# Retention taken two chunks at a time, with four input tiles in place of three

## The chip, the cores and the metric

The kernel runs on one core of a Trainium2 chip. A core has a matrix engine (TensorE, PE in the profile; its weight loads are shown apart, as PEld), a vector engine (VectorE, DVE), a scalar engine (ScalarE, ACT), GpSimd (POOL) and a sync engine (SP) that issues most of the transfers. Each engine runs its own list of instructions in order and waits on semaphores for the others. The metric is the time of one execution on the device, in microseconds; the median of several runs is compared.

## The reference

Three stages follow one another. The first is a retention (a linear attention with decay) over q, k, v of shape 2 x 8 x 768 x 64, in float32; then a feed-forward layer on the 1536 tokens, then a mixture of 8 experts whose gate is normalised eight times over.

```python
for t in range(S):                       # S = 768
    state = gamma * state + einsum('bhd,bhe->bhde', k[:, :, t], v[:, :, t])
    y[:, :, t] = scale * einsum('bhd,bhde->bhe', q[:, :, t], state)
x = y as (1536, 512)
h = x @ w_in;  g = h * clip(h + 3, 0, 6) / 6;  x = g @ w_out
out = sum over experts e of  P[:, e] * (relu(x @ w1[e]) @ w2[e])   # P: gate, 8 rounds of normalisation
```

## The kernel before

The change touches the retention alone, which is the first 54 us of 1268. The two batches are cut into 6 chunks of 128 tokens each, 12 chunks in all, numbered 0 to 11; chunks 0 and 6 begin a batch. For each chunk there are two input tiles of 512 KB: qk (queries and keys with the head dimension on the rows, four pairs of heads) and kv (keys and values with the tokens on the rows). The work of one chunk n is:

- scores: 16 matmuls, keys against queries, on 64 rows of the array each, two side by side, into the PSUM banks s0 and s1; VectorE multiplies both by the decay mask into two tiles a (L391).
- within: 16 matmuls of a with the values, 64 columns of the array each, two side by side, into a bank y (L416).
- across: 8 matmuls of the full array, the scaled queries qs with the copied state rs of the chunks before, added into the same y (L422). A batch's first chunk has none.
- state: 8 matmuls of the full array, scaled keys ks with the values, added into one PSUM bank r for the whole batch (L401); ScalarE copies the diagonal blocks to rs, one of two tiles that take turns (L407). A batch's last chunk has none.
- GpSimd makes ks from kv (L375) and qs from qk (L368).
- keep empties y: ScalarE writes the rounded high part (L309), VectorE the difference as low part (L311), and from chunk 4 on ScalarE copies y a second time into tiles b11 to b22 (the list late, L429).

Each of the PSUM tags s0, s1, y and r has two banks that take turns. The instructions are given in a hand-written order, and each engine's list follows it. Beside the retention VectorE and ScalarE split the 64-bit weights of the feed-forward layer into two parts; pump(n) puts n such steps (one VectorE operation each: L243, L155, L248, L175 in turn) at that place of the order, and the step at L155 asks for the next raw tile on SP's queue. The list HP says how many steps go with each chunk, 18 in all.

Before, the loop goes chunk by chunk: scores of chunk n + 1, its qs, the loads of qk, then within, across, keep and state of chunk n, ks of chunk n + 1, the load of kv, and pump. The scores thus run one chunk ahead. qk and kv have three buffers each, so a load waits on SP until the tile three chunks earlier has been used. After the loop comes the dense stage, whose first matmuls are at L483: x0 with the split weights into banks s0, then x1 into banks y, and the second product into acc (L587).

Of the kernel before, what the change touches and what calls it, by code (L numbers as in the profile page):

```python
# [23 lines left out]
NPAIR = H // 2  # L24
NCB = S // P
NCH = B * NCB
# [20 lines left out]
TURN = (4, 9, 14)  # L47
GATE = lambda it, at: 16 * it + at > 7 and (16 * it + at) % 24 in (2, 8, 14, 19)
APART = 3
KVB = 3  # L50
QKB = 3
WARM = 12
HP = (1, 1, 1, 2, 2, 1, 1, 2, 2, 2, 2, 2)
AHEAD = 3
RAWS = (0, 2)
GF = 4
NGR = F1T // GF
PLAIN = 1
# [6 lines left out]
def kernel(  # L65
# [11 lines left out]
    nc = tc.nc  # L77
# [5 lines left out]
    def bank(tag, name=None):  # L83
        return ps_s.tile([P, BLK], F32, tag=tag, name=name or tag)

    by_pair = lambda t: t.rearrange("p (h i) -> p h i", h=NPAIR)
# [17 lines left out]
    wg_raw = const.tile([P, KT, E], F32, name="wg_raw")  # L104
# [28 lines left out]
    def load_w(tag=None):  # L133
        unit = next(raw_next, None)
        if unit is None:
            return
        i, part = unit
        tags[unit] = tag = tag or next(ring["raw"])
        t = sp.tile([P, 2 * BLK], U32, tag=tag, name="raw")
        nc.sync.dma_start(out=t, in_=wf_in[i, :, part * BLK:(part + 1) * BLK].bitcast(U32))  # L140
        raw_t[unit] = t
# [130 lines left out]
    def rounded():  # L272
        while later:
            later.pop(0)()
# [3 lines left out]
    def pump(n):  # L278

        for _ in range(n):  # L280
            rounded()
            if not next(split_next, False):
                break
            state_["pumped"] += 1
# [17 lines left out]
    def keep(n, y):  # L302

        b, at_ = divmod(n * P, BLK)
        cs = slice(at_, at_ + P)
        pieces = [(x0[0], x0[1], y)] if b == 0 else [(x1[0], x1[1], y)] if b == 1 else [
            (x3[0], x3[1], y[:, 0:2]), (x2[0], x2[1], y[:, 2:4])]
        for hi, lo, src in pieces:
            nc.scalar.activation(out=hi[:, :, cs], in_=src, func=AF.Copy)  # L309
        for hi, lo, src in pieces:  # L310
            nc.vector.tensor_tensor(out=lo[:, :, cs], in0=src, in1=f32(hi[:, :, cs]), op=ALU.subtract)  # L311
        if b:
            late.extend((t[:, :, cs], y[:, 2 * k:2 * k + 2]) for k, t in enumerate(((b11, b21), (b12, b22))[b - 1]))
# [4 lines left out]
    qk_t, kv_t, qs_t, ks_t, a_t, acc_r = {}, {}, {}, {}, {}, {}  # L318
# [5 lines left out]
    rs = [at1.tile([P, NPAIR, P], F32, name=f"rs{i}") for i in range(2)]  # L324

    def load_qk(n):
        if n < NCH:
            qk_t[n] = at2.tile([P, 2, NPAIR, P], F32, tag="qk", name="qk", bufs=QKB)
            nc.sync.dma_start(out=qk_t[n], in_=qk_in[n])

    def spread(tag, to, row):

        t = by_pair(bank(tag, "dm"))
        nc.tensor.matmul(
            t.rearrange("p h i -> p (h i)"), tab[:, to * P:(to + 1) * P], tab[:, TO + row * BLK:TO + (row + 1) * BLK],
            start=True, stop=True,
        )  # L340
        return t
# [13 lines left out]
    def query_table(c, tag):  # L355

        nc.scalar.activation(out=tq[:, c - 1], in_=spread(tag, 2, c), func=AF.Copy)

    def load_kv(n):
        if n < NCH:  # L360
            kv_t[n] = at2.tile([P, 2, DM], F32, tag="kv", name="kv", bufs=KVB)
            nc.sync.dma_start(out=kv_t[n], in_=kv_in[n])

    def scale_q(n):
        c = n % NCB
        if c and n < NCH:
            t = at2.tile([P, NPAIR, P], F32, tag="qs", name="qs")
            nc.gpsimd.tensor_tensor(out=t, in0=qk_t[n][:, 0], in1=tq[:, c - 1], op=ALU.mult)  # L368
            qs_t[n] = t

    def scale_k(n):
        c = n % NCB
        if c < NCB - 1:
            t = at2.tile([P, DM], F32, tag="ks", name="ks")
            nc.gpsimd.tensor_tensor(  # L375
                out=t.rearrange("p (h d) -> p h d", h=H), in0=kv_t[n][:, 0].rearrange("p (h d) -> p h d", h=H),
                in1=gk[:, c].rearrange("p (h o) -> p h o", o=1).to_broadcast([P, H, D]), op=ALU.mult,
            )
            ks_t[n] = t

    def scores(n):
        if n >= NCH:
            return
        t = [by_pair(bank(f"s{j}", "sc")) for j in range(2)]
        for p in range(NPAIR):
            for j in range(2):
                r = slice(j * D, (j + 1) * D)
                nc.tensor.matmul(t[j][:, p], qk_t[n][r, 1, p], qk_t[n][r, 0, p], start=True, stop=True)  # L388
        for j in range(2):
            a_t[n, j] = a = at2.tile([P, NPAIR, P], F32, tag="a", name="a", bufs=4)  # L390
            nc.vector.tensor_tensor(out=a, in0=t[j], in1=dmask[:, j], op=ALU.mult)  # L391

    def state(n):
        b, c = divmod(n, NCB)
        if c == NCB - 1:
            return
        if c == 0:
            acc_r[b] = by_pair(bank("r"))
        for p in range(NPAIR):
            cs = slice(p * P, (p + 1) * P)  # L400
            nc.tensor.matmul(  # L401
                acc_r[b][:, p], ks_t[n][:, cs], kv_t[n][:, 1, cs],
                start=(c == 0 and p == 0), stop=True, skip_group_check=True,
            )
        for j in range(2):
            r = slice(j * D, (j + 1) * D)
            nc.scalar.activation(out=rs[n % 2][r, :, r], in_=acc_r[b][r, :, r], func=AF.Copy)  # L407

    def attend(n):
        c = n % NCB  # L410

        y = by_pair(bank("y"))
        for p in range(NPAIR):
            for j in range(2):
                h = 2 * p + j
                nc.tensor.matmul(  # L416
                    y[j * D:(j + 1) * D, p], kv_t[n][:, 1, h * D:(h + 1) * D],
                    a_t[n, j][:, p], start=(p == 0), stop=(c == 0), skip_group_check=True,
                )
        if c:  # L420
            for p in range(NPAIR):
                nc.tensor.matmul(  # L422
                    y[:, p], rs[(n - 1) % 2][:, p], qs_t[n][:, p],
                    start=False, stop=True, skip_group_check=True,
                )
        keep(n, y)
        state(n)
        for t, src in late:
            nc.scalar.activation(out=t, in_=src, func=AF.Copy)  # L429
        late.clear()  # L430
# [776 lines left out]
    with tc.manual_schedule():  # L1207
# [4 lines left out]
        load_kv(0)  # L1212
        load_kv(1)
        load_qk(2)
        load_w()
        load_kv(2)
        nc.vector.memset(rs[0][:, 0], 0.0)
        nc.vector.memset(rs[0][:, 1:], 0.0)
        nc.vector.memset(rs[1], 0.0)
# [13 lines left out]
        scale_k(0)  # L1233
        for c in (2, 3):
            query_table(c, "y")
        for n in range(NCH):
            scores(n + 1)
            if n == 0:
                for c in range(4, NCB):
                    query_table(c, "r")  # L1240
            scale_q(n + 1)
            if n <= AHEAD:
                load_qk(n + QKB)
            if n >= AHEAD:
                load_qk(n + QKB + 1)
            if n in RAWS:
                load_w()
            attend(n)
            if n + 1 < NCH:
                scale_k(n + 1)  # L1250
            load_kv(n + KVB)
            pump(HP[n])
            if n == 0:
                nc.sync.dma_start(out=wg_raw, in_=wg_in)
        open_["at2"].close()
        open_["at1"].close()

# [35 lines left out]
        def quotas(p, items):  # L1293


            span, load, n = [], [], 0
            for kind, b, f in items:
                span.append(1 if kind == "q" else 2)
                if kind == "q":
                    load.append((0, 0, 0, 1, 1, 2, 2)[n])  # L1300
                    n += 1
                else:
                    load.append(1 if kind == "a" else 5 if f % GF == GF - 1 else 1)
            share = (sum(load) + STEPS_OF[p]) / sum(span)
            out = [0]
            for at in range(len(items)):
                out.append(max(out[-1], min(STEPS_OF[p], round(share * sum(span[:at + 1]) - sum(load[:at + 1])))))
            return out[1:-1] + [STEPS_OF[p]]
# [7 lines left out]
        for p, items in enumerate(phases):  # L1316
            start, quota = state_["pumped"], quotas(p, items)
# [204 lines left out]
```

## Time and profile before

| | |
|---|---|
| median of 3 runs | 1269.07 us (1268.55 to 1269.15) |
| the profiled execution | 1269.38 us |
| its span, first to last instruction | 1267.7 us |
| TensorE busy | 1262.4 us, 100% of the span |
| VectorE busy | 1043.6 us, 82% |
| ScalarE busy | 570.3 us, 45% |
| GpSimd busy | 75.3 us, 6% |
| granted TensorE clock, mean | 1.000 |

The profile is one execution recorded by the hardware. The busy time of TensorE includes modelled ends of matmuls, which overlap; how closely matmuls follow each other is read from their starts. 1.7 us of the execution lie outside the span.

### The profile page before, as it was taken

Reading aid. Unit: us, or ns where it says so; the run is one execution under the profiler, and the core shown is the slowest. Engines: PE = TensorE matmul, PEld = TensorE weight load, DVE = VectorE, ACT = ScalarE, POOL = GpSimd, SP = SyncE. Lnnn points to the kernel's source line nnn. Section 1 sums busy time; section 2 is a strip of 40 time slices with the busy share of each in tenths; the row PEclk is TensorE's granted clock in tenths of the full one; section 3 lists DMA queues with packets and bytes.
Section 4 is the critical chain, followed back from the end, with each engine's and each line's share of the span. In section 5 each row is a group of like instructions: output and inputs, shape, how many; then the busy total and the mean of one; then the engine's idle time right before and its main releaser. Section 6 shows DMA issues by size and latency. Waiting matters only on the chain.

```text
span 1267.7 us, 17330 instructions
## 1 busy us (share of the span) xinstructions
PE 1262.4 (100%) x6565; PEld 1070.3 (84%) x6565; DVE 1043.6 (82%) x1634; ACT 570.3 (45%) x968; POOL 75.3 (6%) x99
## 2 busy tenths in 40 slices
PE   9999999999999999999999999999999999999998
PEld 8888888887899899999988888888888888888887
DVE  5898777767788787777778898989998889998885
ACT  4665545444644544444535433344343344344331
POOL 4321111100000000000000000000000000000000
PEclk9999999999999999999999999999999999999999
DMA  9522222113777777777665354353344443354321
GB/s 330 206 67 88 70 72 66 56 60 139 276 271 268 275 273 275 275 274 275 236 240 156 98 163 146 123 158 91 118 149 142 140 141 108 100 162 145 125 67 67
DMA packets 82287, 205.72 MB, mean 162 GB/s; under 512 B 7750, under 2 KB 32582, under 8 KB 78236
## 3 DMA queue, kind: packets, MB, share of 16 engines
q1 hardware_dynamic: 76860, 144.81, 34.9%
q0 software_dynamic: 5344, 59.80, 12.7%
q8 instruction: 52, 0.85, 0.3%
q14 instruction: 31, 0.25, 0.1%
HBM read 142.69 MB, written 61.90 MB: 161 GB/s over the span
## 4 chain that ended last, share of the span: by engine, by line
PE 98%; DMA 1%; DVE 0%; ACT 0%; issue 0%
PE s L961 33%; PE acc L1088 23%; PE y L1184 14%; PE acc L587 10%; PE r L961 4%; PE y L502 3%; PE s L502 3%; PE s L483 2%; PE y L483 2%; PE acc L1143 2%; PE sc L388 1%; PE y L416 1%; PE y L422 1%; DMA qk<-in_qk 1%; PE r L401 1%; PE y L1227 0%
## 5 line engine op out<-in xcount | busy, mean ns | idle before, releaser
L961 PE MATMUL s<-x,w 128*128 128x256 f32 (+1 forms) x1728 | 325.3, 330 | 0.0
L961 PEld LDWEIGHTS s<-x,w 128*128 128x128 f32 x1728 | 274.8, 189 | 40.4 <-issue 0.8
L1088 PE MATMUL acc<-gh,w 128*128 128x512 f32 x840 | 287.3, 389 | 0.0
L1184 PE MATMUL y<-w,g 128*128 128x512 f32 x768 | 196.8, 393 | 0.0
L1088 PEld LDWEIGHTS acc<-gh,w 128*128 128x128 f32 x840 | 157.7, 188 | 32.8
L1088 PE MATMUL acc<-gl,w 128*128 128x512 f32 x420 | 163.4, 389 | 0.0
L1184 PEld LDWEIGHTS y<-w,g 128*128 128x128 f32 x768 | 136.6, 189 | 22.8
L720 DVE TENSOR_TENSOR c<-acc,c 128x512 f32<-128x512 f32 (+1 forms) x181 | 120.7, 680 | 31.9 <-PE acc L1088 20.7
L961 PE MATMUL s<-xh,w 128*128 128x512 f32 x376 | 130.4, 389 | 0.0
L587 PE MATMUL acc<-ghi,w 128*128 128x512 f32 x384 | 125.6, 390 | 0.0
L717 DVE TENSOR_TENSOR gl<-g,gh 128x1024 fp32r<-128x1024 f32 x94 | 114.2, 1215 | 1.4 <-PE acc L1088 1.1
L714 ACT ACTIVATE gh<-g 128x1024 fp32r<-128x1024 f32 x94 | 99.1, 1055 | 35.0 <-PE acc L1088 34.8
L996 ACT ACTIVATE s<-s 128x256 f32<-128x256 f32 (+1 forms) x64 | 30.4, 476 | 155.5 <-PE s L961 147.2
L1088 PEld LDWEIGHTS acc<-gl,w 128*128 128x128 f32 x420 | 78.8, 188 | 16.3
L714 ACT ACTIVATE w<-s 128x512 fp32r<-128x512 f32 (+2 forms) x94 | 71.3, 761 | 44.4 <-DVE s L723 44.4
L587 PEld LDWEIGHTS acc<-ghi,w 128*128 128x128 f32 x384 | 72.1, 188 | 16.5 <-issue 0.8
L961 PEld LDWEIGHTS s<-xh,w 128*128 128x128 f32 x376 | 70.6, 188 | 14.7
L717 DVE TENSOR_TENSOR w<-s,w 128x512 fp32r<-128x512 f32 (+2 forms) x94 | 80.0, 852 | 0.0
L717 DVE TENSOR_TENSOR w<-raw,w 128x768 fp32r<-128x768 f32 (+2 forms) x65 | 69.5, 1070 | 6.8 <-ACT w L714 6.7
L587 PE MATMUL acc<-glo,w 128*128 128x512 f32 x192 | 74.8, 389 | 0.0
L996 ACT ACTIVATE g<-s 128x512 f32<-128x512 f32 x64 | 38.3, 599 | 80.2 <-PE s L961 80.2
L961 PE MATMUL s<-xl,w 128*128 128x512 f32 x188 | 73.1, 389 | 0.0
(209 smaller groups left out, 1835.6 us busy)
## 6 DMA issues: line engine op xcount, KB each, us to landing
w<-kept SPq DMA_DIRECT2D x222, 256.0 KB, 4.7
kept<-w POOLq DMA_DIRECT2D x31, 1792.0 KB, 7.0
raw<-in_we SPq DMA_DIRECT2D x64, 512.0 KB, 5.0
raw<-in_wf SPq DMA_DIRECT2D x32, 512.0 KB, 3.9
r<-in_we SPq DMA_DIRECT2D x64, 256.0 KB, 3.5
qk<-in_qk SPq DMA_DIRECT2D x12, 512.0 KB, 6.4
kv<-in_kv SPq DMA_DIRECT2D x12, 512.0 KB, 6.1
pb<-p SPq DMA_DIRECT2D x8, 512.0 KB, 8.2
```

Source lines behind the costliest of these rows:

```text
L388: nc.tensor.matmul(t[j][:, p], qk_t[n][r, 1, p], qk_t[n][r, 0, p], start=True, stop=True)
L483: nc.tensor.matmul(h, w[:, l, ks], x, start=(k == n == 0), stop=(k == KT - 1 and n == 2))
L502: nc.tensor.matmul(out, part(l, k), r[:, k], start=(start and k == n == 0), stop=(stop and k == 1 and n == 2), skip_group_check=True,)
L587: nc.tensor.matmul(acc_b[i], w[:, l, ws], r, start=(at_ == 0 and j == 0), stop=(at_ == GF - 1 and j == 2))
L714: nc.scalar.activation(out=hi, in_=t, func=AF.Copy)
L717: nc.vector.tensor_tensor(out=lo, in0=t, in1=f32(hi), op=ALU.subtract)
L720: nc.vector.tensor_tensor(out=out, in0=a, in1=b, op=ALU.add)
L961: nc.tensor.matmul(bank[:, 0:half(i)], wt[:, l, ks], r[:, k], start=(start and n == 0), stop=(stop and n == 5), skip_group_check=True,)
L996: copy = lambda out, a: nc.scalar.activation(out=out, in_=a, func=AF.Copy)
L1088: nc.tensor.matmul(x[d], l, r, start=(fresh and a == 0), stop=(a == 5), skip_group_check=True)
L1143: nc.tensor.matmul(acc[:, cs], l, r[:, cs], start=(a == 0), stop=(a == 11), skip_group_check=True)
L1184: nc.tensor.matmul(acc, l[:, cs], r[:, f % 2], start=(f == 0 and k == 0), stop=(f == 3 and k == 2))
```

## The change

The chunks go in pairs. The scores of both chunks come first, then state and across of both, then within of both, so attend is split into across, within and kept; whichever of across and within comes first for a chunk takes the y bank. y of a pair is emptied (kept) in the next pair, around its scores. Chunks 0 and 1 have an order of their own ahead of the loop, and state 1 and across 1 stand in pair 1. The state of chunk 6, which opens the second batch, is moved into pair 2, in front of that pair's within. qk and kv get four buffers each, and the start loads qk 3, and kv 3 behind the first raw weight tile. The splitting steps go by pairs, 19 in all, in front of a pair's within.

```diff
--- before.py
+++ after.py
@@ -47,12 +47,11 @@
 TURN = (4, 9, 14)
 GATE = lambda it, at: 16 * it + at > 7 and (16 * it + at) % 24 in (2, 8, 14, 19)
 APART = 3
-KVB = 3
-QKB = 3
+KVB = 4
+QKB = 4
 WARM = 12
-HP = (1, 1, 1, 2, 2, 1, 1, 2, 2, 2, 2, 2)
-AHEAD = 3
-RAWS = (0, 2)
+HP = (0, 3, 4, 4, 4, 4)
+RAWS = (0, 1)
 GF = 4
 NGR = F1T // GF
 PLAIN = 1
@@ -392,8 +391,6 @@
 
     def state(n):
         b, c = divmod(n, NCB)
-        if c == NCB - 1:
-            return
         if c == 0:
             acc_r[b] = by_pair(bank("r"))
         for p in range(NPAIR):
@@ -406,25 +403,35 @@
             r = slice(j * D, (j + 1) * D)
             nc.scalar.activation(out=rs[n % 2][r, :, r], in_=acc_r[b][r, :, r], func=AF.Copy)
 
-    def attend(n):
-        c = n % NCB
-
-        y = by_pair(bank("y"))
+    y_t = {}
+
+    def within(n, first):
+
+        if first:
+            y_t[n] = by_pair(bank("y"))
+        y = y_t[n]
         for p in range(NPAIR):
             for j in range(2):
                 h = 2 * p + j
                 nc.tensor.matmul(
                     y[j * D:(j + 1) * D, p], kv_t[n][:, 1, h * D:(h + 1) * D],
-                    a_t[n, j][:, p], start=(p == 0), stop=(c == 0), skip_group_check=True,
+                    a_t[n, j][:, p], start=(first and p == 0), stop=True, skip_group_check=True,
                 )
-        if c:
-            for p in range(NPAIR):
-                nc.tensor.matmul(
-                    y[:, p], rs[(n - 1) % 2][:, p], qs_t[n][:, p],
-                    start=False, stop=True, skip_group_check=True,
-                )
-        keep(n, y)
-        state(n)
+
+    def across(n, first):
+
+        if first:
+            y_t[n] = by_pair(bank("y"))
+        y = y_t[n]
+        for p in range(NPAIR):
+            nc.tensor.matmul(
+                y[:, p], rs[(n - 1) % 2][:, p], qs_t[n][:, p],
+                start=(first and p == 0), stop=True, skip_group_check=True,
+            )
+
+    def kept(n):
+
+        keep(n, y_t.pop(n))
         for t, src in late:
             nc.scalar.activation(out=t, in_=src, func=AF.Copy)
         late.clear()
@@ -1212,8 +1219,10 @@
         load_kv(0)
         load_kv(1)
         load_qk(2)
+        load_qk(3)
+        load_kv(2)
         load_w()
-        load_kv(2)
+        load_kv(3)
         nc.vector.memset(rs[0][:, 0], 0.0)
         nc.vector.memset(rs[0][:, 1:], 0.0)
         nc.vector.memset(rs[1], 0.0)
@@ -1233,25 +1242,60 @@
         scale_k(0)
         for c in (2, 3):
             query_table(c, "y")
-        for n in range(NCH):
-            scores(n + 1)
-            if n == 0:
-                for c in range(4, NCB):
-                    query_table(c, "r")
-            scale_q(n + 1)
-            if n <= AHEAD:
-                load_qk(n + QKB)
-            if n >= AHEAD:
-                load_qk(n + QKB + 1)
-            if n in RAWS:
+        scores(1)
+        scale_q(1)
+        for c in range(4, NCB):
+            query_table(c, "r")
+        within(0, True)
+        kept(0)
+        within(1, True)
+        state(0)
+        scale_k(1)
+        load_qk(4)
+        load_qk(5)
+        load_kv(4)
+        load_w()
+        pump(HP[0])
+        nc.sync.dma_start(out=wg_raw, in_=wg_in)
+        for m in range(1, NCH // 2):
+            n0, n1 = 2 * m, 2 * m + 1
+            c = n0 % NCB
+            if m > 1:
+                kept(n0 - 2)
+            scores(n0)
+            if m > 1:
+                kept(n1 - 2)
+            scores(n1)
+            if c:
+                scale_k(n0)
+                scale_q(n0)
+            scale_k(n1)
+            scale_q(n1)
+            if m == 1:
+                state(1)
+                across(1, False)
+                kept(1)
+                load_kv(5)
+            load_qk(n0 + 4)
+            load_qk(n1 + 4)
+            if c:
+                state(n0)
+                across(n0, True)
+            if c < NCB - 2:
+                state(n1)
+            across(n1, True)
+            if c == NCB - 2 and n1 + 1 < NCH:
+                scale_k(n1 + 1)
+                state(n1 + 1)
+            if m in RAWS:
                 load_w()
-            attend(n)
-            if n + 1 < NCH:
-                scale_k(n + 1)
-            load_kv(n + KVB)
-            pump(HP[n])
-            if n == 0:
-                nc.sync.dma_start(out=wg_raw, in_=wg_in)
+            pump(HP[m])
+            within(n0, not c)
+            within(n1, False)
+            load_kv(n0 + 4)
+            load_kv(n1 + 4)
+        kept(NCH - 2)
+        kept(NCH - 1)
         open_["at2"].close()
         open_["at1"].close()
 
```

## Rows read from the trace of the kernel before

**Rows 1.** Page: busy time by engine (us, share, instructions), and the chain's shares.
```profile
PE 1262.4 (100%) x6565; PEld 1070.3 (84%) x6565; DVE 1043.6 (82%) x1634; ACT 570.3 (45%) x968; POOL 75.3 (6%) x99
...
PE 98%; DMA 1%; DVE 0%; ACT 0%; issue 0%
```
**Rows 2.** Windows, length, then busy us by engine, granted clock, DMA share, GB/s.
```profile
20.00:40.00 20.00, 20.00 (x237) 17.81 (x238) 15.66 (x23) 10.91 (x25) 11.20 (x10) 1.00 0.95 340
...
54.00:82.00 28.00, 28.00 (x126) 22.96 (x125) 24.85 (x37) 15.77 (x29) 4.52 (x4) 1.00 0.23 75
```
**Rows 3.** Chain that ended last, one chunk: start us, us, what.
```profile
21.23 1.09 PE sc L388 x16
22.32 1.02 PE y L416 x16
23.34 1.09 PE y L422 x8
24.43 0.89 PE r L401 x8
```
**Rows 4.** Timeline, TensorE: start us, us, operation; in brackets idle time and releaser.
```profile
1.12 5.17 PE L1227 MATMUL y<-rs 128*128 128x128 f32 x24 [1.12 <-DVE rs L1217]
...
10.22 1.09 PE L416 MATMUL y<-a,kv 128*64 128x128 f32 x16
...
17.06 0.97 PEld L388 LDWEIGHTS sc<-qk 64*128 64x128 f32 x16 [0.74 <-DMA qk<-in_qk]
...
54.13 0.47 PE L483 MATMUL s<-x0h,w 128*128 128x512 f32 x1
```
**Rows 5.** Timeline: state of chunk 3 and the copies of it.
```profile
24.27 1.06 PE L401 MATMUL r<-kv,ks 128*128 128x128 f32 x8
...
25.42 0.78 ACT L407 ACTIVATE rs<-r 64x256 f32<-64x256 f32 x2 [0.36 <-PE r L401]
```
**Rows 6.** Transfers up to 25.3 us: total moved, then issues by kind.
```profile
DMA packets 2553, 8.35 MB, mean 330 GB/s; under 512 B 533, under 2 KB 533, under 8 KB 2552
...
qk<-in_qk SPq DMA_DIRECT2D x8, 512.0 KB, 6.4
kv<-in_kv SPq DMA_DIRECT2D x6, 512.0 KB, 7.0
raw<-in_wf SPq DMA_DIRECT2D x3, 512.0 KB, 9.2
```
**Rows 7.** Timeline: the load of kv 6 and the scaling that waits for it.
```profile
25.36 0.33 SPq L362 DMA_DIRECT2D kv<-in_kv  x1
...
30.34 1.05 POOL L375 TENSOR_TENSOR ks<-kv,gk 128x512 f32<-128x512 f32 x1 [4.40 <-DMA kv<-in_kv]
```
**Rows 8.** Timeline: mask multiplies of a chunk, and y of chunk 5 emptied.
```profile
18.25 1.29 DVE L391 TENSOR_TENSOR a<-sc,tables 128x512 f32<-128x512 f32 x2 [0.68 <-PE sc L388]
...
32.66 0.60 ACT L309 ACTIVATE x1h<-y 128x512 fp32r<-128x512 f32 x1 [1.68 <-PE y L422]
33.29 0.69 DVE L311 TENSOR_TENSOR x1l<-y,x1h 128x512 fp32r<-128x512 f32 x1 [0.43 <-ACT x1h L309]
...
34.02 0.66 ACT L429 ACTIVATE e<-y 128x256 f32<-128x256 f32 x2 [0.76 <-DVE x1l L311]
```
**Rows 9.** Timeline: a splitting step beside GpSimd's work, and one alone.
```profile
36.01 1.28 POOL L368 TENSOR_TENSOR qs<-qk,tables 128x512 f32<-128x512 f32 x1
...
36.30 1.54 DVE L248 SCALAR_TENSOR_TENSOR w<-raw,w 128x512 uint32<-128x512 uint32 x1
...
53.33 0.68 DVE L248 SCALAR_TENSOR_TENSOR w<-raw,w 128x512 uint32<-128x512 uint32 x1
```
**Rows 10.** Timeline and chain: low part of the second g block, and its matmuls.
```profile
66.73 1.22 DVE L550 SCALAR_TENSOR_TENSOR glo<-g,ghi 128x512 fp32r<-128x512 f32 x1
...
68.02 2.78 PE acc L587 x12
```

## Prediction

> **What bounds the kernel now.** I read the page first. TensorE is busy for the whole span, and the chain that ended last runs through it for 98% of the span [rows 1]. So the time changes by what the first instruction after the retention is moved by, unless another engine falls behind later. The windows come next [rows 2]: from 20 to 40 us the DMA engines are 0.95 busy at 340 GB/s, so a tile asked for earlier does not arrive much earlier, and from 54 to 82 us VectorE is busy for 24.85 of 28 us, so it has little to give once the retention is over. The chain through the retention [rows 3] shows how a chunk is spent: 1.09 us for scores, 1.02 within, 1.09 across, 0.89 state. The state follows the across part in the same full-array shape and costs 0.89; the other three follow a change of array shape. Four groups at 0.89 are 3.56 of the 4.10 us, so the three changes cost 0.54, or 0.18 each. The timeline gives the interval to be shortened [rows 4]: the first within (chunk 0) starts at 10.22, the first matmul of the dense stage after the retention at 54.13. That is 43.91 us. It holds 42 groups (12 within, 10 each of scores, across and state) at 0.89, 37.4 us; 33 changes of shape at 0.18, 5.9 us; and one wait of 0.74 us for qk of chunk 3 [rows 4]. Sum 44.0: the interval is explained.
>
> **The change part by part.** Everything ahead of 10.22 keeps its order, and the loads it needs (qk 0 and 1, kv 0 and 1) are still first.
>
> *Changes of shape.* After the change, the order is within 0, within 1, state 0, then five pairs of (both scores; states and across; both within). I count 17 changes: four up to the first within of pair 1, one into pair 2, and three for each of pairs 2 to 5 (the last of them leads into the dense stage). 16 fewer at 0.18: **-2.9 us**.
>
> *The wait for qk 3.* That tile was asked for at 8.2 us behind others; now it is the sixth big transfer at the start: **-0.75 us**. Alone, these two would bring 54.13 to 50.5.
>
> *State after state.* Now state(n+1) comes one across group behind state(n). It adds into the same PSUM bank that ScalarE still copies to rs, or the next across reads that rs. The row [rows 5]: state's matmuls end at 25.33 (24.27 + 1.06), the two copies run from 25.42 to 26.20, so 0.87 us behind the end. The across group between is issued in 0.89 but starts about 0.2 before that end, because matmuls overlap, so about 0.28 is missing. Three places (state 2, state 3, across 5): **+0.85 us**; none if ScalarE were quicker, 1.2 if its queue is in the way. In pairs 4 and 5 larger waits cover it.
>
> *State 6, pulled into pair 2.* Pair 2 starts at 10.22 + 13 groups (11.6) + 5 changes (0.9) + two of the waits (0.55) = 23.25. State 6 would start after five groups, one change and a wait: 28.2. It needs ks(6), hence kv tile 6, which is asked for when within 2 has freed its buffer, about 22.5. In front of it are eight qk, six kv and three raw tiles, 17 of 512 KB, exactly those of before [rows 6]; 8.35 MB had arrived by 25.3, and 9.5 MB with tile 6 itself. At the 340 GB/s of [rows 2] the rest takes until 28.7. Bounds: before, it was asked for at 25.36 and GpSimd went on at 30.34 [rows 7]; no gain from asking earlier gives 30.3, the whole 2.9 us gives 27.5. I take 28.8, by the rate. Scaling takes 1.05 us [rows 7], so state 6 starts at 29.95: **+1.75 us** (0.4 to 3.2). Both within groups stand behind it on TensorE, and the next pair behind them. Pair 3 then starts at 29.95 + three groups + two changes = 33.0, and pair 4 after six groups and three changes at 38.9.
>
> *The bank of y(7).* y has two banks. In pair 3 across 7 takes the first and within 6 the second, so across 8, in pair 4, takes the bank of y(7), which is the last to be emptied. Emptying is ScalarE's copy 0.60, VectorE's difference 0.69, ScalarE's second copies 0.66, which wait for the difference [rows 8]. On VectorE this stands behind the four weight-splitting steps of pair 3, then the difference of y(6) and the two mask multiplies of chunk 8 (1.29, [rows 8]). Pair 3 is short (5.9 us) but has VectorE's full load: its second mask multiplies end at 4.4 us after its start, and four steps follow. Such a step takes 0.6 alone, but 1.54 with GpSimd active: it started at 36.30 and ended 0.55 after GpSimd's operation ended at 37.29 [rows 9]. kv 8 is asked for 0.8 before pair 3 starts and, with about 0.5 MB in front, lands about 2.9 after the start; then GpSimd has ks 8, qs 8, ks 9, qs 9 in one row, 1.05 to 1.3 each, and each step waits one of them out: they end at about 5.85, 7.15, 8.85 and 9.2, which is 3.3 us into pair 4. Then 0.62 + 1.29 + 0.64 + 0.7 = 3.25 until the bank is free, 6.55 into pair 4, where across 8 was due at 2.85: 3.7 us. Without any meeting, steps of 0.55 end 0.7 into pair 4 and the wait is 1.1. I take **+3.4 us** (1.1 to 4.9, if kv 8 is late too), near the upper end because the row of the meeting is the nearest one and GpSimd's four operations have no other place.
>
> *Across 11.* Pair 5: difference of y(8), masks of chunk 10 done 2.4 in, difference and second copies of y(9) until 3.8, rs(10) two copies 0.78 until 4.6; across 11 was due at 3.7: **+0.95 us** (0.3 to 1.5).
>
> *At nothing.* One splitting step more (19 for 18) and the later raw tiles: the weights are used from 54 us on. Loads of kv 10 and 11 stand behind a raw load on SP's queue that waits for a splitting step, about 1 us; they are needed over 8 us later. Without that cover they would cost that 1 us. Emptying y(10) and y(11) after the last pair ends about 2.7 us behind it with step 19 done; before, it was 2.9, so VectorE's backlog moves along. Its margin is about 0.3 us: the low part of the second g block ends at 67.95, just ahead of its matmuls at 68.02 [rows 10].
>
> *TensorE's clock.* Both windows show the granted clock at 1.00, the 2.4 GHz level [rows 2]; the 0.74 us wait did not change it. The 24 warm-up matmuls, with nothing before them, took 5.17 us or 0.215 each [rows 4], against 0.89 / 8 = 0.11 for the same shape later. I leave it out of the sum. The Trainium skill ("TensorE: Matmul & The Clock Gate", section "Why this matters for your kernels") advises against gaps in TensorE's work in mid-kernel, since the clock falls to its lower level; no row here shows a gap as long as the one I expect, and by that rule the sum would be that of the third rival.
>
> **Sum:** -2.9 - 0.75 + 0.85 + 1.75 + 3.4 + 0.95 = +3.3 us. The profiled execution took 1269.38, 0.31 above the median of the runs, so 1272.7 beside it and **1272.4** beside the median.
>
> **Rivals.** *The loads and VectorE keep up.* Place: kv 6 and the steps of pair 3. If kv 6 lands by 27.1, and the steps run in GpSimd's gaps, the waits are 0.85, 0, about 0.6 and 0.3, and TensorE is 1.9 us early: 1267.2. For it: a deeper queue at the start, four buffers. Against: DMA engines 0.95 busy before. It decides from a landing at 27.1. *TensorE gains, VectorE does not.* The same, but the dense stage waits for the low part of g, where 0.3 us is spare [rows 10], since VectorE ends the retention with the same work behind it: about no change, 1269. *The clock falls* in the wait before across 8: the warm-up row bounds a fall at 5.17 less 2.67 = 2.5 us; one makes 1274.9, two 1277.4. *The stalls are half as long* (a quicker kv 6, steps that meet GpSimd only twice): -3.65 + 0.85 + 3.05 = +0.25, so 1269.3, no change.
>
> **How the numbers follow.** The measurement can tell about 0.2% (2.5 us) from no change. Forecast with both stalls: 0.47, nearly all of it slower by over 0.2%. Clock fall: 0.10, slower. Half the stalls: 0.20, mostly same. VectorE takes the gain: 0.10, same. All keeps up: 0.13, half of it beyond 2.5 us, which needs that nothing but the 0.85 us is left against 3.65 us. So faster 0.07, same 0.38, slower 0.55. Lower bounds of the three unsure waits (0.4, 1.1, 0.3) give -1.0, or 1268.1; the upper ones (3.2, 4.9, 1.5) +6.8, or 1275.9. Range 1268.0 to 1276.3; the forecast's own is 1271 to 1276.
>
> **What would show it.** Right: 17 changes of shape; a wait of state 6 for GpSimd's ks, itself behind kv; a wait of across 8 for ScalarE's second copies; the dense stage starting near 57.4; VectorE's steps ending with GpSimd's operations. Wrong: dense stage before 54, kv 6 landing by 27, or across 8 starting less than 3.5 us into its pair.

## The result, and the profile after

Median 1275.69 us after the change (six executions, 1272.97 to 1277.99), 1269.01 before; ratio 1.0051, 95% interval 1.0036 to 1.0065. Slower by some 6.7 us, and with a spread of 5 us where the kernel before spreads over 1. The time goes with the mean granted clock of TensorE: the two executions at 1272.97 have 1.000 and 0.999 (a mean of 0.999 can hold one short fall: the profile of the run with 5, 5, 2, 3, 4 steps, further down, has 3.4 us at half clock and 0.999), the others 0.998 (1275.31), 0.997 (1276.08, 1276.16) and 0.996 (1277.99). The last is the one profiled, so its rows hold the change's waits and the clock's falls together.

Page after: busy time by engine, and the chain's shares, as in [rows 1].

```profile
PE 1265.7 (99%) x6565; PEld 1075.3 (84%) x6565; DVE 1045.3 (82%) x1634; ACT 569.9 (45%) x968; POOL 75.9 (6%) x99
...
PE 98%; DVE 1%; DMA 1%; issue 0%; ACT 0%; POOL 0%
```

The instructions are the same in number, and still the chain is TensorE's. VectorE now has 1% of it. The timeline after, TensorE's groups and what released those that waited; it answers to [rows 3, 4, 5, 7]:

```profile
10.66 2.00 PE L416 MATMUL y<-a,kv 128*64 128x128 f32 x32
...
19.82 0.97 PEld L398 LDWEIGHTS r<-kv,ks 128*128 128x128 f32 x8 [0.25 <-issue]
...
23.70 2.06 PE L387 MATMUL sc<-qk 64*128 64x128 f32 x32
...
29.74 1.04 POOL L374 TENSOR_TENSOR ks<-kv,gk 128x512 f32<-128x512 f32 x1 [4.96 <-DMA kv<-in_kv]
...
30.84 2.08 PE L398 MATMUL r<-kv,ks 128*128 128x128 f32 x8 [1.89 <-POOL ks L374]
...
35.35 2.06 PE L387 MATMUL sc<-qk 64*128 64x128 f32 x32
...
41.21 2.06 PE L387 MATMUL sc<-qk 64*128 64x128 f32 x32
...
46.10 1.13 PE L427 MATMUL y<-qs,rs 128*128 128x128 f32 x8 [1.74 <-ACT e L436]
...
48.66 2.05 PE L398 MATMUL r<-kv,ks 128*128 128x128 f32 x8 [1.43 <-issue]
...
59.93 1.13 PE L427 MATMUL y<-qs,rs 128*128 128x128 f32 x8 [0.56 <-issue]
...
62.88 0.50 PE L490 MATMUL s<-x0h,w 128*128 128x512 f32 x1
```

Pairs 2, 3 and 4 start at 23.70, 35.35 and 41.21. Four groups waited: state 6 (30.84) for its scaled keys, these for kv 6; across 8 (46.10) for ScalarE's second copies; state 9 (48.66); across 11 (59.93). The dense stage starts at 62.88, 8.75 later than in [rows 4], and the execution is 8.61 longer than the profiled one before. So nothing is lost or won back afterwards. 0.44 of the 8.75 lies ahead of the first within (10.66 for 10.22), whose start differs from one profile to the next, 9.43 to 10.66 over the kernels here; a difference of less than about 1 us between the dense starts of two profiles proves little by itself.

Windows after: length, busy us by engine, granted clock, DMA share, GB/s; the last answers to the second of [rows 2].

```profile
29.00:31.00 2.00, 0.16 (x1) 0.17 (x1) 0.17 (x1) 0.00 (x0) 1.04 (x1) 0.93 1.02 408
31.00:36.00 5.00, 5.00 (x50) 4.60 (x52) 1.35 (x3) 2.57 (x5) 2.26 (x2) 0.69 0.27 98
...
44.00:49.00 5.00, 1.82 (x13) 1.50 (x12) 4.98 (x10) 2.44 (x7) 0.00 (x0) 0.88 0.65 247
49.00:54.00 5.00, 5.00 (x32) 4.78 (x33) 2.33 (x4) 1.96 (x4) 4.14 (x3) 0.50 0.33 114
...
63.00:91.00 28.00, 28.00 (x124) 23.17 (x125) 24.87 (x37) 16.14 (x29) 4.51 (x4) 1.00 0.17 58
```

Behind each of the two long waits the clock is at 0.50, the 1.2 GHz level: about 3.4 us around 31 to 34 and about 6.8 us from 47.9 on. At half speed that costs 1.7 and, without the 0.8 us in which TensorE stood anyway, some 3.0 us. 1277.99 less 4.7 is 1273.3, near the 1272.97 of the execution at 1.000. So of the 8.6 us in the profiled execution a little over half is the clock, the rest the waits less what the pairs save. In the window from 29 TensorE is busy for 0.16 of 2 us, in the one from 44 for 1.82 of 5: it stands idle, and VectorE is busy throughout the latter (4.98 of 5).

What VectorE, GpSimd and ScalarE did between 39 and 49 us after the change:

```profile
39.42 1.27 POOL L367 TENSOR_TENSOR qs<-qk,tables 128x512 f32<-128x512 f32 x1
39.54 1.70 DVE L154 SCALAR_TENSOR_TENSOR w<-raw,w 128x512 uint32<-128x512 uint32 x1
40.93 1.21 POOL L374 TENSOR_TENSOR ks<-kv,gk 128x512 f32<-128x512 f32 x1 [0.24 <-DMA kv<-in_kv]
41.16 1.53 DVE L247 SCALAR_TENSOR_TENSOR w<-raw,w 128x512 uint32<-128x512 uint32 x1
...
42.10 1.72 POOL L367 TENSOR_TENSOR qs<-qk,tables 128x512 f32<-128x512 f32 x1
...
42.61 1.76 DVE L174 TENSOR_TENSOR w<-w 128x512 fp32r<-128x512 f32 x1
...
44.63 0.68 DVE L310 TENSOR_TENSOR x1l<-y,x1h 128x512 fp32r<-128x512 f32 x1
...
45.34 0.66 ACT L436 ACTIVATE e<-y 128x256 f32<-128x256 f32 x2 [2.23 <-DVE x1l L310]
...
47.24 0.66 ACT L436 ACTIVATE e<-y 128x256 f32<-128x256 f32 x2 [0.76 <-DVE x1l L310]
47.79 0.77 ACT L404 ACTIVATE rs<-r 64x256 f32<-64x256 f32 x2
```

As in [rows 9], the first three of pair 3's four steps end half a microsecond behind a GpSimd operation, each 1.5 to 1.8 us long. So the difference of y(6) comes at 44.63, its second copies end at 46.0, and across 8 starts at 46.10. The second copies of y(7) end at 47.9; rs(8) stands behind them on ScalarE, and state 9 behind rs(8).

### The profile page after: what moved, and what is told of

Read it like the earlier page. It is cut to its first block, busy times and chain, and to the rows that moved or that the text cites. A ratio compares the mean times of both kernels' runs of the same rounds, so it can differ in the third digit from the quotient of the medians.

```text
span 1276.2 us, 17315 instructions
## 1 busy us (share of the span) xinstructions
PE 1265.7 (99%) x6565; PEld 1075.3 (84%) x6565; DVE 1045.3 (82%) x1634; ACT 569.9 (45%) x968; POOL 75.9 (6%) x99
## 4 chain that ended last, share of the span: by engine, by line
PE 98%; DVE 1%; DMA 1%; issue 0%; ACT 0%; POOL 0%
PE s L968 33%; PE acc L1095 22%; PE y L1191 14%; PE acc L594 10%; PE r L968 3%; PE y L509 3%; PE s L509 3%; PE s L490 2%; PE y L490 2%; PE acc L1150 2%; PE y L416 1%; PE r L398 1%; PE y L427 1%; PE sc L387 1%; DMA kv<-in_kv 1%; PE y L1236 0%
```

## The experiments

My theory was that of the prediction: the order in pairs saves TensorE 3.6 us, and waits that come from VectorE's queue and from kv 6 cost more; the clock falls when TensorE stands. The rivals: the pairs' own form costs, whatever the waits; or the waits are only a symptom of VectorE's load, and one that is taken away comes back elsewhere. All twelve kernels were timed against the kernel before on the same chip, whose medians lay between 1268.96 and 1269.15. Line numbers from L430 on shift by a few in kernels with helpers.

**State 6 back in pair 3**

```diff
             scores(n0)
+            if not c:
+                scale_k(n0)
+                state(n0)
             ...
-            if c == NCB - 2 and n1 + 1 < NCH:
-                scale_k(n1 + 1)
-                state(n1 + 1)
```

> State 6 goes back into pair 3, between its two groups of scores; all else as after the change. If the loss is made of waits of TensorE: the wait of state 6 for kv 6 (1.9 us in the profile after) goes, two more changes of array shape cost 0.36, so the dense stage starts about 1.5 us earlier, and the slow stretch of the clock behind that wait (3.4 us at half speed) goes too; executions between 1271.5 and 1274.7 in place of 1273.0 to 1278.0. If VectorE's backlog sets the start of the dense stage, TensorE only waits longer in pair 4 and the time stays as after the change.

Measured 1274.73 (1274.13 to 1275.75), ratio 1.0044 (1.0031 to 1.0058). Its timeline, TensorE:

```profile
43.69 1.13 PE L427 MATMUL y<-qs,rs 128*128 128x128 f32 x8 [2.26 <-ACT e L436]
...
46.26 2.05 PE L398 MATMUL r<-kv,ks 128*128 128x128 f32 x8 [1.44 <-POOL ks L374]
```

State 6 no longer waits, and its clock fall is gone. But across 8 waits 2.26 in place of 1.74, state 9 waits as long as before, and all five executions have the mean clock of one long fall (0.997), as the profiled one has behind state 9. Of the 1.9 us, 0.5 came back before across 8 and 0.4 went into the two changes of shape. The dense stage starts at 60.59, 2.29 earlier than after the change, of which some 1.6 is the clock fall that is gone. So the wait and the slow stretch went as expected; of the 1.5 us earlier start about 0.7 is seen, less than two single profiles can tell, and with short waits of 0.62 and 0.51 us in pair 1 that the profile after the change does not have.

**Steps out of pair 3**

```diff
-HP = (0, 3, 4, 4, 4, 4)
+HP = (0, 3, 4, 0, 6, 6)
```

> The four weight-splitting steps of pair 3 go to pairs 4 and 5 (0, 3, 4, 0, 6, 6 steps); all else as after the change. If across 8 and state 9 wait because the emptying of y(6) and y(7) stands behind those steps on VectorE: across 8 loses its wait of 1.7 us, state 9 keeps some 0.6 of 1.4 us, the slow clock stretch of 6.4 us goes; executions between 1270.5 and 1272.3. If the work is only moved, the same waits come back in pair 5 or as a later start of the dense stage's second blocks, and the time stays at 1273 or more.

Measured 1276.70 (1274.58 to 1278.82), ratio 1.0062 (1.0049 to 1.0075), so not better. Timeline, TensorE in pairs 4 and 5:

```profile
43.98 1.13 PE L398 MATMUL r<-kv,ks 128*128 128x128 f32 x8 [0.50 <-issue]
...
53.24 1.13 PE L427 MATMUL y<-qs,rs 128*128 128x128 f32 x8 [2.27 <-issue]
...
55.93 2.04 PE L427 MATMUL y<-qs,rs 128*128 128x128 f32 x8 [1.56 <-issue]
```

Without steps in pair 3, across 8 does not wait at all and state 9 waits 0.50: those steps did cause the wait. But now, behind the six steps of pair 4, across 10 and 11 wait 2.27 and 1.56, and the clock falls there. The second rival, that a wait taken away comes back elsewhere, holds for the total.

**No steps from pair 3 on**

```diff
-HP = (0, 3, 4, 4, 4, 4)
+HP = (0, 3, 4, 0, 0, 0)
```

> After the change, but pairs 3 to 5 hold no weight-splitting step (7 in all in place of 19); the other 12 come in the dense stage. If VectorE's queue makes the waits in pairs 4 and 5: across 8 and across 10 start without a wait, state 9 waits 0.6 at most, the dense stage starts at about 54.5 us or, with the first clock fall, 56.5; what follows is that VectorE, with 7 to 10 us more to do there, holds TensorE up in the dense stage, by 5 us or more. If the waits come from elsewhere, they stay.

Measured 1281.66 (1280.33 to 1281.92), ratio 1.0096 (1.0083 to 1.0110). Waits of TensorE from 36 to 110 us (us in total, times, longest):

```profile
PE y L509 <- DVE g L478: 4.7, 1, 4.7
...
PE y L427 <- issue: 0.6, 1, 0.6
PE r L398 <- issue: 0.5, 1, 0.5
```

In pairs 4 and 5 only 0.5 and 0.6 us are left, and the dense stage starts at 55.80 in spite of the wait for kv 6. Then TensorE waits 4.7 us at once for VectorE in the dense stage, 1.1 for ScalarE and 0.5 for VectorE again, and the clock falls there for 6.8 us: work put off was paid for there, with more than it had cost. The waits in pairs 4 and 5 are VectorE's queue, and that work has no free place later.

**Raw tile 3 behind kv 6**

```diff
-RAWS = (0, 1)
+RAWS = (0, 2)
```

> The third raw weight tile is asked for one pair later, so that it is no longer in front of kv 6; all else as after the change. If kv 6 is late because 9.5 MB have to be moved first, 0.52 MB less at about 0.4 MB per us brings it 1.3 us earlier: state 6 waits 0.6 in place of 1.9 us, time 1.3 us less, more where the clock then holds. If its delay runs from its own request (6.8 us), it lands as before and nothing changes.

Measured 1274.11 (1272.77 to 1275.44), ratio 1.0042 (1.0030 to 1.0055). Timeline:

```profile
27.14 1.04 POOL L374 TENSOR_TENSOR ks<-kv,gk 128x512 f32<-128x512 f32 x1 [2.60 <-DMA kv<-in_kv]
...
28.51 1.06 PE L398 MATMUL r<-kv,ks 128*128 128x128 f32 x8
...
32.61 0.43 DVE L242 TENSOR_SCALAR w<-raw 128x512 uint32<-128x512 uint32 x1 [0.57 <-DMA raw<-in_wf]
...
36.29 1.97 PE L416 MATMUL y<-a,kv 128*64 128x128 f32 x32 [0.73 <-ACT e L436]
...
43.04 1.13 PE L427 MATMUL y<-qs,rs 128*128 128x128 f32 x8 [1.71 <-ACT e L436]
45.61 1.13 PE L398 MATMUL r<-kv,ks 128*128 128x128 f32 x8 [1.44 <-issue]
```

kv 6 is there at 27.14 in place of 29.74, and state 6 does not wait: its delay came from the transfers in front of it. The gain is twice the 1.3 us that the tile's size and the rate explain; where the other half comes from is open. Yet the profiled execution, at full clock, took 1272.77 against 1272.97 for the change at full clock. Now a step waits for raw tile 3 (32.61), the differences of y(4) and y(5) stand behind it, and within 6 waits 0.73; across 8, state 9 and across 11 wait 1.71, 1.44 and 0.92 again. Here the waits before across 8 and state 9 are those of the profile after the change (1.74, 1.43), and the clock did not fall: state 9 takes 1.13 us, not 2.05. So such a wait can be followed by a fall and need not be.

**Copies to rs first**

```diff
-                kept(n1 - 2)
+                kept(n1 - 2, False)      # no second copies here
             ...
                 state(n0)
+                copies()                 # second copies of y
                 across(n0, True)
+            copies()
```

> After the change, but ScalarE's second copies of a pair's second y stand behind the copies of the state to rs, not ahead of them. If state 9 waits because rs(8) stands behind the second copies of y(7), its wait falls from 1.4 to about 0.3 us: undisturbed executions at 1271.9 in place of 1273.0, and a shorter second slow stretch. If state 9 waits for anything else, no change.

Measured 1273.26 (1272.65 to 1275.39), ratio 1.0035 (1.0023 to 1.0048). State 9 no longer waits and the clock holds in the profiled execution (1272.98), but that time is the change's own at full clock. The chain that ended last shows where it went (start us, us, what):

```profile
40.27 1.68 DVE w L174
41.95 0.34 DVE w L242
42.29 0.60 DVE x1l L310
42.89 1.20 DVE a L390 x2
44.10 0.69 DVE x1l L310
...
```

It runs along VectorE from 34.15 to 51.95 without a break: steps, differences and masks one behind the other, the steps stretched beside GpSimd. Across 8 still waits 1.15, and across 10 now waits 1.06.

**Fillers in the waits, long and short**

```diff
+    def fill(k):
+        t = by_pair(bank("r", "fill"))
+        for _ in range(k):
+            nc.tensor.matmul(t[:, 0], dmask[:, 0, 0], dmask[:, 0, 0], start=True, stop=True)
             ...
+                fill(14)                 # ahead of state 6; short: 8
+                fill(12)                 # ahead of across 8; short: 7
+                fill(10)                 # ahead of state 9; short: 6
```

> Filler matmuls (128 columns of a constant into an unused bank) stand in front of state 6 (14), across 8 (12) and state 9 (10), about 1.1 to 1.6 us each, less than the waits there; the waits stay. If the slow clock stretches come from TensorE standing idle, the granted clock stays at 1.00, and all executions fall between 1272.5 and 1273.8, with none at 1275 or above. If the clock falls for another reason, the spread of 1273 to 1278 stays.

> As the run with fillers, but 8, 7 and 6 filler matmuls, each of which issues two 0.11 us parts: 1.8, 1.55 and 1.35 us, now inside the waits of 1.9, 1.7 and 1.4 us. If idle TensorE makes the clock fall and the first fillers only cost what they were longer than the waits (3.0 us): all executions between 1272.5 and 1273.5, clock 1.00. If fillers cost time as such, or the clock falls anyway: 1274 or more.

Long: 1275.87 (1275.73 to 1276.48), all five executions at clock 1.000. Windows of it:

```profile
29.00:36.00 7.00, 7.00 (x93) 6.71 (x93) 1.69 (x4) 2.55 (x5) 3.31 (x3) 1.00 0.64 223
44.00:54.00 10.00, 10.00 (x112) 9.71 (x112) 7.75 (x13) 5.06 (x13) 4.97 (x7) 1.00 0.44 163
```

TensorE is busy all the time, the clock stays, the spread shrinks from 5.0 to 0.75 us. I had miscounted: a filler issues two parts, so they took 3.13, 2.68 and 2.23 us, 3.0 more than the waits of 1.89, 1.74 and 1.43; 1272.97 + 3.0 is 1275.97, against 1275.87 measured. Short: 1273.81 (1273.38 to 1274.74), all at 1.000, somewhat over the 1273.5 expected. So the clock falls because TensorE stands, and the falls are the greater part of what lies between 1273 and 1278; times up to 1274.7 come without one, as the short fillers show.

**Four tiles alone, and with later steps**

```diff
-KVB = 3
-QKB = 3
+KVB = 4
+QKB = 4
             ...
-        load_w()
-        load_kv(2)
+        load_qk(3)
+        load_kv(2)
+        load_w()
+        load_kv(3)
```

> The kernel before, chunk by chunk, with four qk and kv buffers and the first loads in the new order (qk 3 sixth, kv 3 behind the first raw tile). The term for qk 3 says 0.7 us less than before, 1268.3, with no wait of the scores of chunk 3. If that wait is hidden or another load takes its place: 1269.0.

> The chunk-by-chunk order with four buffers and the new first loads, and no splitting step with chunks 0 and 1 (0, 0, 1, 2, 2, 2, 2, 2, 2, 2, 2, 1, again 18). With four tiles alone, the first step waited 3.5 us for its raw tile and held the masks of chunk 3 behind it. If that is what took the 0.7 us of qk 3 back: no wait of TensorE before 20 us, 1268.3. If another wait follows: 1269.0 to 1269.5 as with four tiles alone.

Both are the kernel before in its own order. Alone: 1269.45 (1268.60 to 1269.66), ratio 1.0001 (0.9992 to 1.0010). Timeline:

```profile
15.76 1.20 DVE L243 TENSOR_SCALAR w<-raw 128x512 uint32<-128x512 uint32 x1 [3.51 <-DMA raw<-in_wf]
```

qk 3 is in time, but the first step waits 3.51 us for the raw tile that now comes behind it, and the masks behind the step; within 2 waits 0.45 for them. With later steps (HP = 0, 0, 1, 2, 2, 2, 2, 2, 2, 2, 2, 1) no such wait is left. These are 18 steps; the kernel before has 19, as its list adds up and its trace shows, so this run leaves one more to the dense stage. Timeline, TensorE and one row of VectorE:

```profile
53.37 0.48 PE L483 MATMUL s<-x0h,w 128*128 128x512 f32 x1
...
67.67 0.69 DVE L471 SCALAR_TENSOR_TENSOR g<-g,y 128x512 f32<-128x512 f32 x1 [1.87 <-ACT g L469]
...
81.30 0.50 PE L502 MATMUL y<-x1h,w 128*128 128x512 f32 x1 [0.42 <-DVE g L471]
```

The dense stage starts 0.76 us earlier than in [rows 4], 0.50 of it because the first within does (9.72 for 10.22). Yet the time is 1269.71 (1269.16 to 1270.44), ratio 1.0006 (0.9997 to 1.0014): at 81.30 TensorE waits for VectorE and is 0.2 ahead of the kernel before (81.52). VectorE runs without a break from 67.67 to 79.9, but had stood 1.87 us before that, behind ScalarE, which waited for a GpSimd addition of 2.85 us (1.07 in the kernel before). So what TensorE gains is lost in the chain of the other engines. How much of that is the step more, and how much VectorE's load as such, is not told apart.

**Everything at once, in three steps**

```diff
-HP = (0, 3, 4, 4, 4, 4)
+HP = (0, 5, 5, 2, 3, 4)
             ...
-            pump(HP[m])
             within(n0, not c)
             within(n1, False)
             load_kv(n0 + 4)
             load_kv(n1 + 4)
+            pump(HP[m])
```

To this come the edits of state 6 and of the copies to rs, as above. The second of the three has HP = (0, 3, 6, 2, 4, 4), the third (0, 3, 5, 2, 4, 5).

> Pair order with the three causes treated at once: state 6 between the scores of pair 3, the copies to rs ahead of a pair's last second copies, and the splitting steps spread over the pairs as 5, 5, 2, 3, 4, asked for behind the pair's loads of kv, so that GpSimd and VectorE meet less in pairs 3 and 4. If VectorE's queue was the limit: waits of at most 1 us in pairs 4 and 5, no clock fall, dense stage near 53.3, time 1268.0 to 1269.5. If pairs can't feed TensorE whatever the place of the steps: waits of 2 us or more return in some pair, 1271 or more.

1274.00 (1272.86 to 1275.42), ratio 1.0041 (1.0028 to 1.0055): the five steps of pair 1 hold up y(2) and y(3), and in pair 2 both across groups wait. Timeline:

```profile
28.09 1.13 PE L427 MATMUL y<-qs,rs 128*128 128x128 f32 x8 [1.47 <-DVE x0l L310]
29.88 1.79 PE L427 MATMUL y<-qs,rs 128*128 128x128 f32 x8 [0.66 <-DVE x0l L310]
```

Across 5 takes 1.79 us in place of 1.1: the clock falls here behind waits of 1.47 and 0.66.

> As the run with 5, 5, 2, 3, 4 steps, but 3, 6, 2, 4, 4: pair 1 keeps its load, pair 2 takes one more, pair 4 one more. By VectorE's queue: pair 5 starts with one step more in front of its first y, 0.6 to 1.5 us more waiting there than in the other, 1268.5 to 1270.5. If the place of the steps doesn't matter: the same time as the other.

1272.05 (1270.96 to 1273.65), ratio 1.0024 (1.0015 to 1.0034). Only one long wait is left. Timeline:

```profile
34.80 0.66 ACT L440 ACTIVATE e<-y 128x256 f32<-128x256 f32 x2 [0.76 <-DVE x1l L310]
35.34 0.77 ACT L404 ACTIVATE rs<-r 64x256 f32<-64x256 f32 x2
...
36.22 1.13 PE L398 MATMUL r<-kv,ks 128*128 128x128 f32 x8 [2.72 <-POOL ks L374]
```

The view names GpSimd, whose operation ended at 35.23; the copies of state 6 to rs ended at 36.11, and they had stood behind the second copies of y(4), which stood behind VectorE's six steps. State 7 adds into the bank being copied. This is the longest wait of TensorE ahead of the dense stage in any of these profiles, and the clock did not fall behind it: the granted mean is 1.000 and state 7 takes 1.13 us.

```diff
+                kept(n0 - 2, c > 0)      # pair 3: second copies of y(4) later
                 ...
                 state(n0)
+                copies()
```

> As the run with 3, 6, 2, 4, 4 steps, but 3, 5, 2, 4, 5, and in pair 3 the copies of state 6 to rs stand ahead of the second copies of y(4), behind which they waited until 35.3 us. If that is why state 7 waited 2.7 us: its wait falls below 0.7, the clock holds in most executions, and the dense stage starts at 53.2 to 54.0, as early as or earlier than before the change (54.13). The time then tells which engine decides: if TensorE, 1268.2 to 1269.0; if VectorE, which ends the retention with its steps and two y to empty and is busy without a pause in the dense stage's first blocks, 1269.2 to 1270.5 in spite of the early start, with TensorE waiting for VectorE near 60 to 85 us.

1269.63 (1268.54 to 1269.96), ratio 1.0003 (0.9994 to 1.0012): back at the time before, and the wait is gone. Timeline, TensorE:

```profile
51.20 1.13 PE L427 MATMUL y<-qs,rs 128*128 128x128 f32 x8 [0.85 <-issue]
...
54.16 0.50 PE L494 MATMUL s<-x0h,w 128*128 128x512 f32 x1
```

The dense stage starts where it did before (54.13), a little later than expected, and TensorE does not wait in it. So this run does not show VectorE deciding in the dense stage. From the first within (10.42) it takes 43.74 us, against 43.91 before: 14 changes of shape fewer and the wait for qk 3 are worth 3.3 us, and nearly as much goes into waits of 0.85 us and less that the pairs still have. That speaks in part for the first rival: even without a long wait this form saves nothing. No kernel here beats the one before.

## Why the prediction was right

The direction, the places and most sizes of the waits held; the clock, left out of the sum, is most of what the forecast lacks: +3.3 us forecast, +6.7 measured in the median, +4.0 in the execution with the clock held (1272.97). The range's upper end, 1275.9 by its sum, was made of longer waits at full clock. The waits came out near the forecast, so it is luck that a median lengthened by the clock still lies inside.

- *Changes of shape:* pair 3 takes 5.86 us (35.35 to 41.21) against 5.88 by the sum, so 0.18 per change held.
- *qk 3:* from the first within to pair 2 it takes 13.04 us (10.66 to 23.70), 13.03 by the sum, so both this term and the two short state waits (0.25 measured for 0.28) held. In the old order the same loads take the wait away too, but the time stays, as the two runs with four tiles showed.
- *State 6:* 1.89 measured for 1.75, and the reason held: less in front, earlier there. (The 29.95 is 0.1 more than 28.8 and 1.05 give; nothing hangs on it.)
- *The bank for across 8:* the sum held, the place did not. I had 3.4 us on across 8, for y(7)'s bank; it took y(6)'s and waited 1.74, and state 9 waited 1.43 behind y(7)'s second copies and rs(8): 3.17. It shows in the order: across 8 starts at 46.10, behind y(6)'s second copies and ahead of y(7)'s. The steps of pair 3 ended at 44.7, 9.35 us into the pair, for 9.2 worked out from [rows 9], and y(7) was free 6.69 us into pair 4, for 6.55. That the two waits add up to the one forecast rests on rs(8) standing behind the same copies, which the prediction did not have.
- *Across 11:* 0.56 for 0.95, the one wait that was clearly over-sized.
- *One splitting step more* was not there: the kernel before has 19 steps as well, not 18. The term stood at nothing, so the sum is the same.
- *The clock* was left out of the sum. The forecast of 1272.4 is near the time at full clock (1272.97); the median of 1275.69 lies in the prediction's third rival, the clock fall, which I gave 0.10 with 1274.9 for one and 1277.4 for two. The dense stage starts at 62.88 for the 57.4 expected; less the 4.7 us of the clock that is 58.2. The Trainium skill ("TensorE: Matmul & The Clock Gate", section "Why this matters for your kernels") advises against gaps in TensorE's work in mid-kernel, since the clock falls to its lower level. That was the better guide here than the 0.74 us wait that had left the clock alone: with the waits filled the clock held in ten executions of ten. But not each gap has a fall; one of 2.72 us had none. The bound of 2.5 us per fall was too low for the second (about 3.0).
- *TensorE gains, VectorE does not,* the prediction's second rival, was not what happened after the change, as TensorE was late itself. It bears on a start ahead of 54 us. From the first matmul of the dense stage to the last instruction it takes 1213.3 to 1213.4 us in the nine profiles that start the stage at 55.8 or later and have no long wait in it, 1213.5 to 1213.6 in the three that start it between 54.13 and 54.18, and 1214.1 in the one that starts it at 53.37: the earlier the start, the less of it is handed on. Which engine holds it up there is shown for that one run only, and there it is the chain of VectorE, ScalarE and GpSimd.

Left open: why the clock falls behind such a wait in one execution and not in another. Two executions of the change in six came out at 1272.97, their waits not recorded; but the profiles of other kernels, where the waits are on record, have waits of 1.71 and 1.44 us, of 2.04 and of 2.72 without a fall, and of 1.47 and 0.66 with one. Left open too is what share of VectorE's stretched steps could be had back by moving GpSimd's multiplications, which wasn't tried.

## What to carry to other kernels

Before regrouping TensorE's work to save its changes of shape, count what the other engines must do per group, in order, with the durations they have beside each other: here 3.6 us saved met an engine whose queue had no room, and much of what was taken away in one place came back in a later one, until three edits and another spread of the steps together brought the old time back. When producer and consumer move closer (state behind state, second copies ahead of rs), the short copies between them come onto the path, and their place in the copying engine's queue matters more than their length. In these runs waits of TensorE of 1.5 to 2.7 us cost another 1.6 to 3 us through the clock in some executions and nothing in others, so look at the granted clock of each execution when times begin to spread.

## What the runs showed of the hardware

In the profiled execution after the change the granted clock went to 0.50 behind waits of 1.89 us and of 1.74 and 1.43 us with 0.9 us of work between, and stayed there for about 3.4 and 6.8 us though TensorE was busy again; other executions of the same program kept 1.000 and 0.999. The length of the wait alone did not decide: waits of 1.47 and 0.66 us had a fall behind them (the run with 5, 5, 2, 3, 4 steps), waits of 1.71 and 1.44 (raw tile 3 later), of 2.04 (no steps from pair 3 on) and of 2.72 us (3, 6, 2, 4, 4 steps) had none. With the waits filled the mean stayed at 1.000 ten times out of ten.
